# Another order of the up and down products in the second layer of a spectral mixture-of-experts kernel

## The chip, the cores and the metric

The kernel runs on one core of a Trainium2 chip. The metric is the device time of one execution in microseconds (us). The time of a kernel is the median of its runs.

## The reference, cut to what matters

The input `x` (8, 3072, 256) is filtered along its sequence in the frequency domain. A mixture of eight experts (one expert per token, hidden width 1024) follows, and then a dense second layer. Only this second layer is touched by the change:

```
def _moe2_ref(x, w_in, w_out):          # x: 24576 x 256
    h = np.maximum(x @ w_in, 0.0)       # 24576 x 2048
    return (h * h @ w_out)              # 24576 x 256
```

Everything is float32. The kernel keeps float32 accuracy by splitting each operand into a high and a low part and by forming three products of parts (high by high, low by high, high by low) for each product of the formula.

## The kernel before, in words

The program has three stages: the Fourier filter, the expert layer (the function that issues its steps is `steps_m`, which goes on with the second layer), and the second layer. The second layer works on 48 tiles of 512 tokens (`NTILE2`), and each tile in 8 **units** (`NU`) of 256 hidden columns, so there are 384 units. All engines follow one order, which is the order in which the generators `up2`, `split_h`, `down2` and `split_t` issue their instructions; each engine has its own queue and takes its instructions in that order.

**Up (`up2`, lines 892 to 925).** A unit's 256 x 512 block of `x @ w_in` is formed with a Strassen-like scheme from seven products of 128 x 128 by 128 x 256. Each product (`prod`, line 897) is three matmuls of 256 columns, 21 in all. I name a product by its PSUM tile and the number of its weight block: V0, G3, P1, V4, G6, V5, V2, in the order of the code. The three PSUM tiles are V (pool `psH`, two buffers; the trace calls it `ph`), G (pool `psX`, one buffer, `px`) and P (pool `psH2`, one buffer, `ph`). V4, V5 and V2 add onto what V0 left in V, and G6 adds onto what G3 left in G. Between two products onto the same tile the partial sum is copied out, and the next product waits for that copy:

- ScalarE copies V after V0 into `s1` (line 906), G after G3 into `p5` (line 908), V after V4 into `u2` (line 913), and V after V2 into `C[:, 2]` (line 921).
- VectorE adds P and `s1` into `C[:, 0]` (line 911), V (after V5) and `p5` into `C[:, 3]` (line 917), G (after G6) and `u2` into `C[:, 1]` (line 918).

So V4 waits for the copy `s1`, G6 for the copy `p5`, V5 for the copy `u2`, and V2 for the sum `C[:, 3]`. After V2 and its copy VectorE forms `q`, the square of the positive part of `C` (line 923, 1024 columns).

**Split (`split_h`, lines 927 to 934).** ScalarE casts `q` to the high part `hh` (line 930), and VectorE forms the low part `hl` (line 932).

**Down (`down2`, lines 936 to 961).** 24 matmuls of 256 columns add the unit's part of `h*h @ w_out` onto two PSUM banks (`py`). The sum over a tile's 8 units stays in these banks; behind the last unit ScalarE copies it out (line 951) and GpSimd scatters it to the output (line 954).

**The order before (lines 1055 to 1072).** In step n the up products of unit n, the split of unit n-1 and the down matmuls of unit n-2 are interleaved in four parts. On TensorE a step is

```
V0 G3 | 3 down | P1 V4 | 6 down | G6 V5 | 9 down | V2 | 6 down
```

that is 45 matmuls. `split_h` is issued in parts 1 and 2, and one step of `split_t` (lines 858 to 890, the split of the next tile's input, spread over four units of a tile) at the end of a step. The loads of a later tile (`load_t`) go through SyncE's DMA queue at unit 2 of each tile.

Of the kernel before, what the change touches and what calls it, by code (L numbers as in the profile page):

```python
# [17 lines left out]
ALU = mybir.AluOpType  # L18
# [84 lines left out]
def spectral_moe_kernel(ctx: ExitStack, tc: tile.TileContext, x, filt_r, filt_i, w_gate, w_og, w1, w2,  # L103
                        w_in, w_out, c_ma, c_mi, c_mb, c_mb2, c_sg, c_cum, out):
    nc = tc.nc
# [608 lines left out]
    def py_tiles(t):  # L714
        return [pl["psY2" if t % 2 and "psY2" in pl else "psY"].tile([128, TT], F32, name=f"py{h}") for h in range(2)]
# [82 lines left out]
    def up(t, f):  # L798
        xh, xl = X[t]
        w = width[t]  # L800
        h1, l1 = (a[:, 0] for a in W[t, f // 2])
        f2 = f % 2
        ps = ph_tile()[:, 0:w]
        n = 0
        for c in range(2):
            for a, b in ((h1, xh), (h1, xl), (l1, xh)):
                nc.tensor.matmul(ps, a[:, c, f2 * 128:(f2 + 1) * 128], b[:, c, 0:w], start=n == 0, stop=n == 5)  # L807
                n += 1
        hh = pl["hp"].tile([128, TT], F32R, name="hh")[:, 0:w]
        hl = pl["hp"].tile([128, TT], F32R, name="hl")[:, 0:w]  # L810
        nc.scalar.activation(hh, ps, AF.Relu)  # L811
        tick[:] = [hh[0:1, 0:1].bitcast(F32)]
        nc.vector.scalar_tensor_tensor(hl, ps, 0.0, hh.bitcast(F32), op0=ALU.max, op1=ALU.subtract)  # L813
        H[t, f] = hh, hl
# [77 lines left out]
    def up2(t, u):  # L892

        bh, bl, _ = X2[t]
        wsh, wsl = w2nd[0:2]

        def prod(ps, a, b, start):
            for n, (x, y) in enumerate(((wsh, bh), (wsh, bl), (wsl, bh))):
                nc.tensor.matmul(ps, x[:, u, a], y[:, b], start=start and n == 0, stop=n == 2, skip_group_check=True)  # L899

        bank = lambda name: pl[name].tile([128, TT], F32, name="px" if name == "psX" else "ph")[:, 0:256]
        V, G, P = bank("psH"), bank("psX"), bank("psH2")
        s1, p5, u2 = (pl["sp"].tile([128, 256], F32, name=n) for n in ("s1", "p5", "u2"))
        C = pl["cp"].tile([128, 4, 256], F32, name="C")
        prod(V, 0, 0, True)
        nc.scalar.copy(s1, V)
        prod(G, 3, 3, True)
        nc.scalar.copy(p5, G)
        yield
        prod(P, 1, 1, True)  # L910
        nc.vector.tensor_tensor(C[:, 0], P, s1, ALU.add)
        prod(V, 4, 4, False)
        nc.scalar.copy(u2, V)
        yield
        prod(G, 6, 2, False)
        prod(V, 5, 5, False)
        nc.vector.tensor_tensor(C[:, 3], V, p5, ALU.add)  # L917
        nc.vector.tensor_tensor(C[:, 1], G, u2, ALU.add)
        yield
        prod(V, 2, 6, False)  # L920
        nc.scalar.copy(C[:, 2], V)  # L921
        q = pl["cp"].tile([128, 4, 256], F32, name="q")
        nc.vector.scalar_tensor_tensor(q, C, 0.0, C, op0=ALU.max, op1=ALU.mult)  # L923
        H2[t, u] = q
        yield

    def split_h(t, u):
        q = H2[t, u]
        hh, hl = (pl["h2p"].tile([128, 4, 256], F32R, name=n) for n in ("hh2", "hl2"))
        nc.scalar.copy(hh, q)  # L930
        yield
        nc.vector.tensor_tensor(hl, q, hh.bitcast(F32), ALU.subtract)  # L932
        H2[t, u] = hh, hl
        yield

    def down2(t, u):

        hh, hl = H2[t, u]
        woh, wol = w2nd[2:4]
        if u == 0:  # L940
            Z[t] = [p.rearrange("p (c d) -> p c d", c=2) for p in py_tiles(t)]
        for m in range(24):
            k, i, c, n = m // 12, m // 6 % 2, m // 3 % 2, m % 3
            x, w = ((hh, woh), (hl, woh), (hh, wol))[n]
            nc.tensor.matmul(Z[t][k][:, c, :], x[:, 2 * i + k, c * 128:(c + 1) * 128], w[:, 2 * u + i, :],  # L945
                             start=u == 0 and m in (0, 12), stop=u == NU - 1 and m in (11, 23), skip_group_check=True)
            if u == NU - 1 and m in (11, 23):
                if k == 0:
                    Z[t].append(pl["oup"].tile([128, 4, D], F32, name="ou"))
                ou = Z[t][2]  # L950
                nc.scalar.copy(ou[:, 2 * k:2 * k + 2, :], Z[t][k])  # L951
                io = X2[t][2]
                for c in range(2 * k, 2 * k + 2):
                    nc.gpsimd.indirect_dma_start(out=outv[4 * t + c], out_offset=bass.IndirectOffsetOnAxis(ap=io[:, c:c + 1], axis=0),  # L954
                                                 in_=ou[:, c, :], in_offset=None)
            if m in (2, 8, 17):
                yield
        del H2[t, u]
        if u == NU - 1:
            del X2[t], Z[t]  # L960
        yield
# [3 lines left out]
    units2 = [(t, u) for t in range(NTILE2) for u in range(NU)]  # L965
# [3 lines left out]
    def step_1(t, f):  # L969

        last = t + 1 == KP
        if f == 5 and t + 2 == KP:
            start_t(KP)
        if f == 1 and t + 1 >= KP:
            for n in (t + 2, t + 3) if last else (t + 3,):
                if n < NMAIN:
                    start_t(n)
        if f == 1 and last:
            gather(KP)
        if f == 3 and t + 2 < NMAIN and t + 2 != KP:  # L980
            gather(t + 2)
        if f % 2 == 1:

            g = NQ * t + f // 2 + 2
            if NQ * KP <= g < NQ * NMAIN:
                split_w(*divmod(g, NQ))
            if NQ * KP <= g + 2 < NQ * NMAIN:
                load_w(*divmod(g + 2, NQ))
        if t + 1 < NMAIN:
            at = (4, 5, 7) if last else (2, 4, 6)  # L990
            if f == at[0]:
                scale_x(t + 1)
            if f == at[0] + 1:
                put_ids(t + 1)
            if f in at[1:]:
                turn_x(t + 1, at.index(f) - 1)
        elif f == 1:
            load_t(0)
            load_t(1)
        if f not in (1, 5) and dec and next(dec[0], 0) == 0:  # L1000
            dec.clear()
            dcs.close()
            pl["bp0"] = ctx.enter_context(tc.tile_pool(name="bp0", bufs=1))
            pl["bp0"].tile([128, 16], F32, name="pad0")
        if t + 1 == NMAIN and f >= 3:
            if f == 3:
                first.append(split_t(0))
            next(first[0], None)

    def extra(t):  # L1010

        start_t(t)
        gather(t)
        for q in range(3):
            load_w(t, q)
        scale_x(t)
        put_ids(t)
        turn_x(t, 0)
        turn_x(t, 1)
        for f in range(NF + 1):  # L1020
            if f < NF:
                if f % 2 == 0:
                    split_w(t, f // 2)
                    if f == 0:
                        load_w(t, 3)
                up(t, f)
            if f:
                down(t, f - 1)

    def rest(t):  # L1030

        if t < NTILE1:
            with tc.If(used[0] > slot[t - KP]):
                extra(t)
                rest(t + 1)
# [3 lines left out]
    def steps_m():  # L1039
        for n in range(len(jobs) + LAG1):  # L1040
            if n < len(jobs):
                t, f = jobs[n]
                up(t, f)
                step_1(t, f)
            if n >= LAG1:
                down(*jobs[n - LAG1])
            yield
        used.append(nc.values_load(usedi[0:1, 0:1], min_val=0, max_val=NTILE_T))
        with tc.If(used[0] > NTILE_T - NX):
            extra(NMAIN)  # L1050
            rest(NMAIN + 1)
        m1.close()
        xgs.close()
        open_m2()
        st = iter(())
        for n in range(len(units2) + 2):
            g = up2(*units2[n]) if n < len(units2) else iter(())
            t, u = units2[min(n, len(units2) - 1)]
            d = down2(*units2[n - 2]) if n >= 2 else iter(())
            for part in range(4):  # L1060
                next(g, None)
                if part == 0 and 0 < n <= len(units2):
                    sh = split_h(*units2[n - 1])
                if part in (1, 2) and n:
                    next(sh, None)
                next(d, None)
            if u == 2 and t + 2 < NTILE2:
                load_t(t + 2)
            if u == 3 and t + 1 < NTILE2:
                st = split_t(t + 1)  # L1070
            next(st, None)
            yield
# [43 lines left out]
    m = steps_m()  # L1116
# [4 lines left out]
    for i, k in enumerate(order):  # L1121
# [3 lines left out]
        n = done["a"]  # L1125
# [62 lines left out]
```

## Time and profile before

| | |
|---|---|
| median of 3 runs | 3807.01 us (3805.06 to 3810.75) |
| the profiled execution's own time | 3809.94 us |
| its span, first to last instruction | 3808.2 us |
| TensorE busy in the span | 98% |
| VectorE, ScalarE, GpSimd busy | 72%, 52%, 16% |
| mean granted TensorE clock | 0.997 |

The second layer fills the time from 1777 us to the end. TensorE is always busy there by its records, which says little, because a matmul's record (some 0.28 us) is longer than the distance from its start to the next one's start (some 0.115 us): matmuls overlap. What has to be read is that distance, called the **pitch** below.

### The profile page before, as it was taken

What the parts mean: (1) busy time and instruction counts of PE and PEld (TensorE: products, weight loads), DVE (VectorE), ACT (ScalarE), POOL (GpSimd) and SP (SyncE); (2) the same over time, 40 slices, a digit from 0 to 9 for tenths busy, and PEclk for the clock granted to TensorE, in tenths of its full rate; (3) what the DMA queues carried; (4) which work ended last, traced back from release to release, by engine and by line L of the source; (5) the groups of instructions that cost most, each with busy time, mean ns of one, the idle gap of its engine ahead of it and who ended that gap; (6) DMA issues with size and microseconds to landing.
All of it is one profiled execution on the core that took longest, in us unless ns stands there. A gap on an engine that the chain in (4) does not pass through costs nothing.

```text
span 3808.2 us, 73021 instructions
## 1 busy us (share of the span) xinstructions
PE 3750.1 (98%) x27156; PEld 3501.1 (92%) x27156; DVE 2759.2 (72%) x5024; ACT 1966.4 (52%) x3896; POOL 607.0 (16%) x641
## 2 busy tenths in 40 slices
PE   8999999999999999999999999999999999999998
PEld 7888877888888888888999999999999999999998
DVE  6677685678878875656777777777777777777775
ACT  6466473354545454554555555555555555555554
POOL 3477574000000000000011001000100110011001
PEclk9999999999999999999999999999999999999999
DMA  6333322455555554543000100010000001000100
GB/s 193 101 114 116 105 81 95 149 161 165 174 159 176 165 165 154 158 159 95 24 26 27 29 23 29 23 29 23 29 24 28 24 29 29 23 26 26 29 18 18
DMA packets 259756, 306.63 MB, mean 81 GB/s; under 512 B 74721, under 2 KB 203202, under 8 KB 259394
## 3 DMA queue, kind: packets, MB, share of 16 engines
q1 hardware_dynamic: 239936, 249.75, 21.6%
q0 software_dynamic: 18432, 51.93, 3.8%
q8 instruction: 214, 3.51, 0.4%
q14 instruction: 148, 1.21, 0.1%
q10 hardware_dynamic: 1026, 0.23, 0.0%
HBM read 221.63 MB, written 80.19 MB: 79 GB/s over the span
## 4 chain that ended last, share of the span: by engine, by line
PE 84%; issue 10%; DVE 2%; POOL 1%; DMA 1%; ACT 1%; another core or an unknown queue 0%; DVEq 0%; POOLq 0%; ACTq 0%; SPq 0%
PE py L945 22%; PE ph L899 14%; PE ph L807 14%; PE py L824 14%; PE px L899 6%; PE o L360 3%; PE p L380 3%; PE o L394 2%; PE p L281 2%; PE p L334 1%; PE p L338 1%; PE p L309 1%; POOL out_dram L954 1%; PE px L787 1%; DMA xt<-in_x_dram 0%
## 5 line engine op out<-in xcount | busy, mean ns | idle before, releaser
L945 PE MATMUL py<-woh,hh 128*128 128x256 f32 x3072 | 857.2, 279 | 0.0
L945 PE MATMUL py<-woh,hl 128*128 128x256 f32 x3072 | 852.8, 278 | 0.4 <-DVE hl L932 0.4
L945 PE MATMUL py<-wol,hh 128*128 128x256 f32 x3072 | 852.9, 278 | 0.0
L954 POOL DMA_INDIRECT out_dram<-ou,ix x192 | 213.2, 1110 | 2912.9 <-ACT ou L951 2869.0
L945 PEld LDWEIGHTS py<-woh,hl 128*128 128x128 f32 x3072 | 579.9, 189 | 0.9 <-DVE hl L932 0.8
L945 PEld LDWEIGHTS py<-woh,hh 128*128 128x128 f32 x3072 | 579.9, 189 | 0.0
L945 PEld LDWEIGHTS py<-wol,hh 128*128 128x128 f32 x3072 | 576.3, 188 | 0.0
L899 PE MATMUL ph<-bh,wsh 128*128 128x256 f32 x1920 | 540.9, 282 | 5.9 <-DMA ytd<-yt 4.6
L811 ACT ACTIVATE hh<-ph 128x512 fp32r<-128x512 f32 (+1 forms) x464 | 248.7, 536 | 574.8 <-PE ph L807 548.8
L899 PE MATMUL ph<-bl,wsh 128*128 128x256 f32 x1920 | 537.1, 280 | 0.0
L899 PE MATMUL ph<-bh,wsl 128*128 128x256 f32 x1920 | 536.7, 280 | 0.0
L923 DVE SCALAR_TENSOR_TENSOR q<-C 128x1024 f32<-128x1024 f32 x384 | 470.5, 1225 | 6.4 <-ACT C L921 6.4
L932 DVE TENSOR_TENSOR hl<-q,hh 128x1024 fp32r<-128x1024 f32 x384 | 467.1, 1216 | 1.1 <-ACT hh L930 1.1
L813 DVE SCALAR_TENSOR_TENSOR hl<-ph,hh 128x512 fp32r<-128x512 f32 (+1 forms) x464 | 283.3, 611 | 252.0 <-ACT hh L811 244.2
L917 DVE TENSOR_TENSOR C<-ph,p 128x256 f32<-128x256 f32 x384 | 163.6, 426 | 412.8 <-ACT hh L930 402.5
L921 ACT COPY C<-ph 128x256 f32<-128x256 f32 x384 | 143.4, 373 | 532.4 <-PE ph L899 500.2
L930 ACT CAST hh<-q 128x1024 fp32r<-128x1024 f32 x384 | 402.8, 1049 | 1.3 <-DVE q L923 1.3
L899 PEld LDWEIGHTS ph<-bh,wsh 128*128 128x128 f32 x1920 | 362.3, 189 | 7.1 <-issue 4.7
L899 PEld LDWEIGHTS ph<-bl,wsh 128*128 128x128 f32 x1920 | 360.9, 188 | 0.0
L899 PEld LDWEIGHTS ph<-bh,wsl 128*128 128x128 f32 x1920 | 360.8, 188 | 0.0
L824 PE MATMUL py<-hh,wh 128*128 128x512 f32 (+1 forms) x928 | 336.6, 369 | 0.0
L807 PE MATMUL ph<-xh,wh 128*128 128x512 f32 (+1 forms) x928 | 335.2, 361 | 0.0
(265 smaller groups left out, 8045.4 us busy)
## 6 DMA issues: line engine op xcount, KB each, us to landing
r<-in_moe_w_dram SPq DMA_DIRECT2D x440, 256.0 KB
xt<-in_x_dram SPq DMA_DIRECT2D x48, 512.0 KB
r<-ytd SPq DMA_DIRECT2D x48, 512.0 KB
xg<-srt SPq DMA_DIRECT2D x41, 544.0 KB
ytd<-yt SPq DMA_DIRECT2D x41, 512.0 KB
xg<-srt SPq DMA_DIRECT2D x17, 272.0 KB
ytd<-yt SPq DMA_DIRECT2D x17, 256.0 KB
raw<-in_moe_w_in_dram SPq DMA_DIRECT2D x16, 256.0 KB
```

Source lines behind the costliest of these rows:

```text
L807: nc.tensor.matmul(ps, a[:, c, f2 * 128:(f2 + 1) * 128], b[:, c, 0:w], start=n == 0, stop=n == 5)
L811: nc.scalar.activation(hh, ps, AF.Relu)
L813: nc.vector.scalar_tensor_tensor(hl, ps, 0.0, hh.bitcast(F32), op0=ALU.max, op1=ALU.subtract)
L824: nc.tensor.matmul(Y[t][h], a[:, f % 2, h * 128:(h + 1) * 128], b, start=f == 0 and i == 0, stop=f == NF - 1 and i == 2, skip_group_check= ...
L899: nc.tensor.matmul(ps, x[:, u, a], y[:, b], start=start and n == 0, stop=n == 2, skip_group_check=True)
L917: nc.vector.tensor_tensor(C[:, 3], V, p5, ALU.add)
L921: nc.scalar.copy(C[:, 2], V)
L923: nc.vector.scalar_tensor_tensor(q, C, 0.0, C, op0=ALU.max, op1=ALU.mult)
L930: nc.scalar.copy(hh, q)
L932: nc.vector.tensor_tensor(hl, q, hh.bitcast(F32), ALU.subtract)
L945: nc.tensor.matmul(Z[t][k][:, c, :], x[:, 2 * i + k, c * 128:(c + 1) * 128], w[:, 2 * u + i, :], start=u == 0 and m in (0, 12), stop=u == ...
L954: nc.gpsimd.indirect_dma_start(out=outv[4 * t + c], out_offset=bass.IndirectOffsetOnAxis(ap=io[:, c:c + 1], axis=0), in_=ou[:, c, :], in_o ...
```

## The change

The generator `up2` yields at more places, `down2` yields after 6 and after 15 of its 24 matmuls instead of after 3, 9 and 18, and the last three pieces of a unit (V2, the copy `C[:, 2]`, the square `q`) are issued in the next step, each behind a piece of the next unit (`old` is the generator of the unit before). The sum `C[:, 1]` is now issued before `C[:, 3]`. In the first step that has down matmuls (n == 2) their first six stand between G3 and P1; in all others the first two groups of down follow each other. A step's order on TensorE becomes

```
V0 (V2 of the unit before) G3 P1 V4 G6 | 15 down | V5 | 9 down
```

Every matmul, copy and sum of before is still issued, once.

```
--- before.py
+++ after.py
@@ up2
         prod(V, 0, 0, True)
         nc.scalar.copy(s1, V)
+        yield
         prod(G, 3, 3, True)
         nc.scalar.copy(p5, G)
         yield
         prod(P, 1, 1, True)
         nc.vector.tensor_tensor(C[:, 0], P, s1, ALU.add)
+        yield
         prod(V, 4, 4, False)
         nc.scalar.copy(u2, V)
-        yield
         prod(G, 6, 2, False)
+        nc.vector.tensor_tensor(C[:, 1], G, u2, ALU.add)
+        yield
         prod(V, 5, 5, False)
         nc.vector.tensor_tensor(C[:, 3], V, p5, ALU.add)
-        nc.vector.tensor_tensor(C[:, 1], G, u2, ALU.add)
         yield
         prod(V, 2, 6, False)
+        yield
         nc.scalar.copy(C[:, 2], V)
+        yield
         q = pl["cp"].tile([128, 4, 256], F32, name="q")
         nc.vector.scalar_tensor_tensor(q, C, 0.0, C, op0=ALU.max, op1=ALU.mult)
@@ down2
-            if m in (2, 8, 17):
+            if m in (5, 14):
                 yield
@@ steps_m
         st = iter(())
+        none = iter(())
+        old = none
         for n in range(len(units2) + 2):
-            g = up2(*units2[n]) if n < len(units2) else iter(())
+            g = up2(*units2[n]) if n < len(units2) else none
             t, u = units2[min(n, len(units2) - 1)]
-            d = down2(*units2[n - 2]) if n >= 2 else iter(())
-            for part in range(4):
-                next(g, None)
-                if part == 0 and 0 < n <= len(units2):
-                    sh = split_h(*units2[n - 1])
-                if part in (1, 2) and n:
-                    next(sh, None)
+            d = down2(*units2[n - 2]) if n >= 2 else none
+            next(g, None)
+            next(old, None)
+            next(g, None)
+            next(old, None)
+            if n == 2:
                 next(d, None)
+            next(g, None)
+            next(old, None)
+            sh = split_h(*units2[n - 1]) if 0 < n <= len(units2) else none
+            next(g, None)
+            next(sh, None)
+            if n != 2:
+                next(d, None)
+            next(d, None)
+            next(g, None)
+            next(sh, None)
+            next(d, None)
+            old = g
```

## Rows read from the trace of the kernel before

**Rows 1.** Page's busy times; a stretch: busy of PE, PEld, DVE, ACT, POOL; clock; DMA.

```profile
PE 3750.1 (98%) x27156; PEld 3501.1 (92%) x27156; DVE 2759.2 (72%) x5024; ACT 1966.4 (52%) x3896; POOL 607.0 (16%) x641
...
2500.00:3000.00 500.00, 500.00 (x4290) 500.00 (x4289) 369.39 (x573) 259.95 (x549) 53.02 (x48) 1.00 0.09 27
```

**Rows 2.** The chain of waits over one unit: start, us, what; from V0 on.

```profile
2505.66 0.35 PE ph L899 x3
2506.02 0.35 PE px L899 x3
2506.37 0.35 PE py L945 x3
2506.72 0.69 PE ph L899 x6
2507.42 0.68 PE py L945 x6
2508.10 0.35 PE px L899 x3
2508.46 0.35 PE ph L899 x3
2508.81 1.06 PE py L945 x9
2509.87 0.35 PE ph L899 x3
2510.23 0.68 PE py L945 x6
```

**Rows 3.** The timeline, same unit: last matmul of G3, copy p5, first weights of G6.

```profile
2506.09 0.28 PE L899 MATMUL px<-bh,wsl 128*128 128x256 f32 x1
...
2506.46 0.37 ACT L908 COPY p<-px 128x256 f32<-128x256 f32 x1
...
2507.83 0.19 PEld L899 LDWEIGHTS px<-bh,wsh 128*128 128x128 f32 x1
```

**Rows 4.** The timeline in unit 1, before any down: V0's last matmul, s1, V4.

```profile
1782.58 0.28 PE L899 MATMUL ph<-bh,wsl 128*128 128x256 f32 x1
...
1782.90 0.37 ACT L906 COPY s<-ph 128x256 f32<-128x256 f32 x1
...
1783.26 0.28 PE L899 MATMUL ph<-bh,wsl 128*128 128x256 f32 x1
1783.32 0.19 PEld L899 LDWEIGHTS ph<-bh,wsh 128*128 128x128 f32 x1
1783.38 0.33 PE L899 MATMUL ph<-bh,wsh 128*128 128x256 f32 x1
...
1783.54 0.28 PE L899 MATMUL ph<-bl,wsh 128*128 128x256 f32 x1
...
1783.78 0.28 PE L899 MATMUL px<-bh,wsh 128*128 128x256 f32 x1
```

**Rows 5.** The timeline where a V2 waited for its sum: one of three such units.

```profile
1816.85 0.19 PEld L899 LDWEIGHTS ph<-bh,wsh 128*128 128x128 f32 x1
...
1817.08 0.28 PE L899 MATMUL ph<-bl,wsh 128*128 128x256 f32 x1
...
1817.19 0.28 PE L899 MATMUL ph<-bh,wsl 128*128 128x256 f32 x1
...
1817.30 0.28 PE L945 MATMUL py<-woh,hh 128*128 128x256 f32 x1
```

**Rows 6.** The page's costliest groups: VectorE's and ScalarE's long steps of a unit.

```profile
L923 DVE SCALAR_TENSOR_TENSOR q<-C 128x1024 f32<-128x1024 f32 x384 | 470.5, 1225 | 6.4 <-ACT C L921 6.4
L932 DVE TENSOR_TENSOR hl<-q,hh 128x1024 fp32r<-128x1024 f32 x384 | 467.1, 1216 | 1.1 <-ACT hh L930 1.1
...
L917 DVE TENSOR_TENSOR C<-ph,p 128x256 f32<-128x256 f32 x384 | 163.6, 426 | 412.8 <-ACT hh L930 402.5
...
L930 ACT CAST hh<-q 128x1024 fp32r<-128x1024 f32 x384 | 402.8, 1049 | 1.3 <-DVE q L923 1.3
```

More of the change, by code (lines that the diff above doesn't have):

```diff
@@ L911, in up2 @@
         nc.vector.tensor_tensor(C[:, 0], P, s1, ALU.add)
+        yield
         prod(V, 4, 4, False)
         nc.scalar.copy(u2, V)
+        prod(G, 6, 2, False)
+        nc.vector.tensor_tensor(C[:, 1], G, u2, ALU.add)
         yield
-        prod(G, 6, 2, False)
         prod(V, 5, 5, False)
         nc.vector.tensor_tensor(C[:, 3], V, p5, ALU.add)
-        nc.vector.tensor_tensor(C[:, 1], G, u2, ALU.add)
         yield
         prod(V, 2, 6, False)
+        yield
         nc.scalar.copy(C[:, 2], V)
+        yield
         q = pl["cp"].tile([128, 4, 256], F32, name="q")
```

## The prediction

> **What bounds the kernel now.** I read the busy times first, then one long stretch, then the chain of waits, then the timeline. In the stretch from 2500 to 3000 us TensorE starts 4290 matmuls, one per 116.6 ns, at a granted clock of 1.00, which is the 2.4 GHz level, while VectorE is busy 74% and ScalarE 52% of the time [rows 1]. The chain of waits names nothing but matmuls there, 45 per unit, in 5.25 us (2505.66 to 2510.23 + 0.68) [rows 2]. So no wait bounds the second layer; the pitch of the matmuls does, and it is all that a new order can win.
>
> The pitch has two values. Six down matmuls take 0.68 us from 2507.42, and again from 2510.23: 113.3 ns each, the fast pitch. The nine from 2508.81 take 1.06 us: 117.8 ns, the slow pitch [rows 2]. All are 256 columns wide, with operands of the same kinds, so it is not the work that differs. Read along the unit, the pitch changes at each step from a down group to an up group and nowhere else: V0 starts a slow stretch that lasts through three down matmuls, P1 brings the fast pitch back, G6 starts the next slow stretch, and V2 ends it [rows 2]. I take that as a rule: **each switch from down to up flips the pitch**. Price of a slow stretch, with the three matmuls that bring the fast pitch back: 2505.66 to 2507.42 is 1.76 us for 15 matmuls, where 15 x 113.3 ns are 1.70, so 60 ns for nine slow matmuls; 2508.10 to 2510.23 is 2.13 us for 18, where the fast pitch gives 2.04, so 90 ns for fifteen [rows 2]. That is about 5 ns per slow matmul and 15 ns for the way back. The check: 45 x 113.3 = 5.10 us, plus 60, plus 90, is the unit's 5.25.
>
> **The change, part by part.**
>
> *Fewer switches.* A step has two flips in place of four, at V5 and at V0. If V0 to G6 and the 15 down matmuls are fast, only V5 and the nine behind it are slow: twelve, 12 x 5 + 15 = 75 ns. The unit would be 5.10 + 0.075 = 5.175 us, 72 ns less than 5.247 (I take 45 x 116.6 ns [rows 1]).
>
> *G6 behind its copy.* Before, 15 matmuls (three down, P1, V4, six down) stand between G3 and G6. Now it is six, P1 and V4. The chain that G6 must wait out is in the trace: G3's last matmul starts at 2506.09 and the copy p5 at 2506.46, 0.37 later, and takes 0.37 [rows 3]; from the end of such a copy to the weight load that waits for it are 0.05 us (1782.90 + 0.37, then 1783.32) [rows 4]. Together 0.79. G6's weight load would come naturally 6 x 113.3 = 0.68 us after G3's last matmul. So TensorE stands for 0.11 us in every unit. The trace has this distance once: in unit 1, with no down matmuls yet, V4 follows V0 after six matmuls (G3, P1). Its weight load comes at 1783.32 where the matmul ahead started at 1783.26, and the matmul after is at 1783.54, 0.16 behind V4's first in place of 0.11 [rows 4]. There the copy started only 0.31 us after the matmul (1782.58 to 1782.90) [rows 4]; in the steady units it is 0.37. Bounds of this wait: 0.05 us [rows 4] and 0.11 us [rows 3]; I take 0.11, the row of the same copy. Nothing else fills it: behind G6's load in TensorE's queue stand 15 down matmuls with all their inputs ready, and they are held with it, as is everything later. ScalarE and VectorE shift along, and they have room.
>
> *What pitch follows that wait.* Where V2 waited in full (weights at 1816.85), the next matmuls came at 1817.08, 1817.19 and 1817.30, the fast pitch [rows 5]. Where V4 waited half as long, the next two came 0.24 us apart (1783.54 to 1783.78), slow [rows 4]. A wait of 0.11 us is a full one (the load comes later than the matmul would have), so I take fast, and no more loss than the wait.
>
> *The other waits,* each with its cover. V4 waits for s1: nine matmuls between, 1.02 us against 0.79. V5 waits for u2: 18 between. V2 waits for VectorE's sum behind V5: 12 between, 1.36 us, against 0.37 + 0.43 [rows 6] + 0.05. The copy of V2 now stands behind p5, so it costs p5 nothing. Counted from G3's last matmul: sum of P at 0.7 to 1.1 us, `q` to 2.4, `hh` to 3.5, the sum of V5 (matmuls at 3.2, sum from 3.6) to 4.0, `hl` to 5.2 [rows 6]; the down matmuls want them in the next step, at 5.3 + 1.1 = 6.4. Cover 1.2 us. In the unit where `split_t` puts four subtractions behind `hl` (some 4 x 0.43 us), `q` and `hh` come 0.8 us later, and the cast behind them (1.05 us) may hold the next s1 by 0.2 to 0.3 us, which leaves V4 some 0.03 us short: 47 tiles, at most 2 us in all. The scatters and SyncE's loads keep their places; GpSimd is busy 16% [rows 1].
>
> *Start and end.* V2 of unit 0 no longer holds unit 1, but `q` of units 0 and 1 comes later for the first down matmuls; at the end six down matmuls fewer cover the last unit's chain (6 x 0.113 = 0.7 us lost). I put both together at 0, within 1 us.
>
> **Sum.** Unit: 5.10 + 0.075 + 0.115 = 5.290 us, 43 ns more than before. Steps 3 to 383 have it, 381 of them: +16.4 us. The profiled execution took 3809.94 us, 2.9 above the median; 3809.9 + 16.4 = 3826.3, and against the median of 3807.0 it is **3823.4 us**, slower by 0.43%.
>
> **Rivals.**
>
> *The flips go the other way,* so that V0 to G6 and the 15 down matmuls are slow: 33 slow matmuls, 33 x 5 + 15 = 180 ns. The wait is then shorter, 0.79 - 6 x 0.118 = 0.08. Unit 5.10 + 0.18 + 0.08 = 5.36: +43 us, 3850. It decides if the wait leaves the slow pitch, as in unit 1 [rows 4]; against it stands the full wait of rows 5.
>
> *The pitch hangs on something else than the switches* (a group's addresses), so it stays at 116.6 ns on average and only the wait is new: 0.79 - 6 x 0.1166 = 0.09 us, +34 us, 3841. For it: I infer the rule from one pattern of groups. Against: the four flips of every unit. [...]
>
> *All fast but for the wait:* if V5's switch does not bring the slow pitch, the unit is 5.10 + 0.115 = 5.215, 32 ns less: -12 us, 3795. While the wait stands, no pitch gives more.
>
> *The wait costs nothing* and the fewer switches win: -72 ns x 381 = -27 us, 3780. This is the faster case, in one mechanism: G6's weights would have to be loaded before p5 is done, so that only the matmul waits. Then the matmul, due 0.79 us after G3's last one (7 x 113.3), comes just as p5 is done; it decides once the load gets ahead by 0.1 us. Against it: in unit 1 the load itself came late, with the matmul behind it [rows 4]. [...]
>
> *The two cancel:* a wait of 0.05 us, as in rows 4, with the 75 ns of slow matmuls gives 5.225, -8 us; a wait of 0.07 gives no change.
>
> **How the numbers follow.** About 0.2% (8 us) is what a measurement of this kernel can tell from no change. My forecast, +10 to +22 us: 0.42. Pitch independent of the switches, or slow after part of the waits, +22 to +38: 0.14. Flips the other way, +38 to +45: 0.12. All fast but for the wait: 0.10. No wait: 0.10. Cancelled: 0.12. Slower by over 0.2% is 0.42 + 0.14 + 0.12 = 0.68; faster 0.20; the same 0.12. The range from 3794 to 3850 leaves out the case without a wait and the edge of the reversed one. The forecast's own range is 3817 to 3829.
>
> **What would show it.** In the profile after, ScalarE's copy p5 should be what ends an idle of G6's weight load, some 380 times, with 0.3 us or less between the matmul ahead and the load; the chain should show 33 fast and 12 slow matmuls per step; V0 of one unit to V0 of the next should be 5.29 us. I am wrong if G6's load comes 0.11 us behind the matmul ahead (no wait), if the nine down matmuls behind V5 take 1.02 us and not 1.06, or if the fifteen take 1.77 us and not 1.70.

## The result, and the profile after

The changed kernel takes 3838.73 us (median of 4 runs, 3834.85 to 3839.97) where the kernel before takes 3808.88 (4 runs): a ratio of 1.0079, with a 95% interval of 1.0066 to 1.0092. It is slower by 29.9 us. The forecast was 3823.4, 16.4 us slower: the direction and the wide range (3794 to 3850) held, the size was off by nearly half, and the time lies outside the forecast's own range of 3817 to 3829.

All of it lies in the second layer. In the profiled executions its first up matmul starts at 1777.4 us before and 1776.1 after, its last down matmul at 3797.4 and 3827.1: 2019.9 us against 2051.1, 31.1 us more. From one V0 to the next a unit takes 5.248 us before and 5.327 after, on the mean of 377 units; 381 x 0.079 us are 30.1 us. (Counts of units, here and below, are of those that start between 1800 and 3808 us, unless steps are named.)

The busy times of the page after, which answer to [rows 1]:

```profile
PE 3781.0 (99%) x27156; PEld 3523.5 (92%) x27156; DVE 2758.9 (72%) x5024; ACT 1996.7 (52%) x3896; POOL 620.1 (16%) x641
```

And the stretch from 2500 to 3000 us of the kernel after: us, then busy time (count) of PE, PEld, DVE, ACT, POOL, granted clock, DMA share, GB/s.

```profile
2500.00:3000.00 500.00, 499.91 (x4228) 497.54 (x4227) 363.36 (x565) 264.00 (x542) 56.64 (x48) 1.00 0.09 27
```

The same number of matmuls in all, the same granted clock of 1.00 (the 2.4 GHz level), but 4228 matmuls in the stretch where there were 4290: 118.3 ns each, not 116.6. TensorE looks busier than before (99%), which shows again that its busy share says little here.

The chain of waits over two units of the kernel after (start, us, what), which answers to [rows 2]. A `ph` group of six right behind nine `py` is V0 and the V2 of the unit before:

```profile
2504.91 0.34 PE px L899 x3
2505.25 0.68 PE ph L899 x6
2505.93 0.46 PE px L899 x3
2506.39 1.77 PE py L949 x15
2508.16 0.35 PE ph L899 x3
2508.51 1.02 PE py L949 x9
2509.53 0.71 PE ph L899 x6
2510.24 0.35 PE px L899 x3
2510.60 0.70 PE ph L899 x6
2511.30 0.43 PE px L899 x3
2511.73 1.70 PE py L949 x15
2513.43 0.36 PE ph L899 x3
2513.78 1.06 PE py L949 x9
```

Read the two units side by side. In the first, G3 (0.34) and P1, V4 (0.68 for six) are fast, and G6 takes 0.46 instead of 0.34, because it waits. Then the 15 down matmuls are slow (1.77), and the nine behind V5 fast (1.02). The second is the mirror: V0 to V4 are slow (0.71, 0.35, 0.70), G6 takes 0.43 instead of 0.35, the 15 down matmuls are fast (1.70), and the nine slow (1.06). So the two switches flip the pitch, as forecast, and the wait is there, as forecast. But the wait itself also turned the pitch over, in both units, where the forecast took fast behind it.

The timeline of these two waits: G3's last matmul, the copy p5, V4's last matmul, G6's first weights and second matmul, then the same of the next unit. It answers to [rows 3].

```profile
2504.98 0.28 PE L899 MATMUL px<-bh,wsl 128*128 128x256 f32 x1
...
2505.34 0.37 ACT L909 COPY p<-px 128x256 f32<-128x256 f32 x1 [0.31 <-PE px L899]
...
2505.66 0.28 PE L899 MATMUL ph<-bh,wsl 128*128 128x256 f32 x1
...
2505.77 0.19 PEld L899 LDWEIGHTS px<-bh,wsh 128*128 128x128 f32 x1
...
2505.99 0.28 PE L899 MATMUL px<-bl,wsh 128*128 128x256 f32 x1
...
2510.32 0.28 PE L899 MATMUL px<-bh,wsl 128*128 128x256 f32 x1
...
2510.69 0.37 ACT L909 COPY p<-px 128x256 f32<-128x256 f32 x1 [0.25 <-PE px L899]
...
2511.11 0.19 PEld L899 LDWEIGHTS px<-bh,wsh 128*128 128x128 f32 x1
...
2511.34 0.28 PE L899 MATMUL px<-bl,wsh 128*128 128x256 f32 x1
```

G6's weights come 0.79 us after G3's last matmul in both units (2504.98 to 2505.77, 2510.32 to 2511.11), which is the sum of the prediction. Because V0 to V4 are fast in the one and slow in the other, the same chain costs 0.108 us in the one and 0.08 in the other (median of 138 and of 239 units; it is read from G6's first matmul to its second).

Sorted by the pitch of V0 to V4, of the 15 down matmuls and of the nine, nearly all of the 377 units are of three kinds: fast, slow, fast (137 units, median 5.313 us); slow, fast, slow (136 units, 5.313 us); slow, slow, fast (102 units, 5.347 us). The kind that the forecast was made for (fast, fast, slow, at 5.290) occurs once. Two of the prediction's own signs of being wrong came: 15 down matmuls at 1.77 us and nine at 1.02, each in at least 239 of the 377 units.

### The profile page after: what moved, and what is told of

Its sections match the earlier page's. It is cut to its first block, busy times and chain, and to the rows that moved or that the text cites. A ratio compares the mean times of both kernels' runs of the same rounds, so it can differ in the third digit from the quotient of the medians.

```text
span 3838.0 us, 72547 instructions
## 1 busy us (share of the span) xinstructions
PE 3781.0 (99%) x27156; PEld 3523.5 (92%) x27156; DVE 2758.9 (72%) x5024; ACT 1996.7 (52%) x3896; POOL 620.1 (16%) x641
## 4 chain that ended last, share of the span: by engine, by line
PE 38%; issue 14%; POOL 2%; ACT 0%; DVE 0%; POOLq 0%; ACTq 0%
PE py L949 20%; PE ph L899 12%; PE px L899 6%; POOL out_dram L958 2%; DVE q L927 0%; ACT p L909 0%; DVE hl L936 0%; ACT hh L934 0%; POOLq L1200 0%; ACT ou L955 0%; DVE C L920 0%; ACT C L924 0%; POOLq L958 0%; DVE C L912 0%; ACTq L955 0%
## 5 line engine op out<-in xcount | busy, mean ns | idle before, releaser
L958 POOL DMA_INDIRECT out_dram<-ou,ix x192 | 225.3, 1173 | 2932.0 <-ACT ou L955 1735.3
L906 ACT COPY s<-ph 128x256 f32<-128x256 f32 x384 | 143.5, 374 | 433.9 <-PE ph L899 369.8
```

## The experiments

The time of the kernel before differs between the chips on which the runs below were made (3809.4, 3793.6, 3795.1 and 3805.1 us). So ratios are given, and the length of the second layer in the trace, which does not hold the stages ahead of it.

**G3 first: the wait taken away.** In the step, V2 of the unit before goes behind G3:

```
             next(g, None)
-            next(old, None)
             next(g, None)
             next(old, None)
+            next(old, None)
```

> G3 and its copy p5 are issued before V2 of the unit before, so nine matmuls (1.02 us) stand between G3 and G6 where the chain through p5 takes 0.79 us. Theory (each switch from down to up flips the pitch, and G6's wait costs its own time and also puts the pitch wrong): no wait, the same pattern in every unit, two flips; with V0 to G6 and 15 down matmuls fast and 12 matmuls slow the unit is 5.175 us, some 3782 us in all, 27 us under the kernel before. If this start gives the other pattern, 33 slow matmuls, the unit is 5.28 us and the time some 3821 us. Rival A (the pitch belongs to a group of matmuls, not to the switches): the time is the same whatever the start, so this run and the next agree. Rival B (only the wait matters, the mean pitch stays 116.6 ns): unit 5.247 us, the time of the kernel before.

Measured: 3788.03 us, a ratio of 0.9943 (0.9926 to 0.9959): faster than both kernels. The second layer is 2002.4 us long, 17.6 less than before. The chain of waits over two units of this one run, the first at 2509.76:

```profile
2509.76 0.35 PE ph L899 x3
2510.11 0.34 PE px L899 x3
2510.45 1.02 PE ph L899 x9
2511.47 0.34 PE px L899 x3
2511.81 1.70 PE py L949 x15
2513.51 0.35 PE ph L899 x3
2513.87 1.06 PE py L949 x9
```

and another, at 2192.67:

```profile
2192.67 0.35 PE ph L899 x3
2193.02 0.35 PE px L899 x3
2193.38 1.06 PE ph L899 x9
2194.44 0.35 PE px L899 x3
2194.79 1.77 PE py L949 x15
2196.56 0.35 PE ph L899 x3
```

The first has up matmuls and 15 down matmuls at the fast pitch, and nine at the slow pitch; the second the reverse. The same instructions, in the same order, on the same tiles: so the pitch does not belong to a group of matmuls (rival A falls), and the mean pitch does not stay (rival B falls). The first pattern has 325 units, with a median of 5.173 us (the theory said 5.175); the second 42 units, 5.267 us (5.28). What keeps the time above the 3782 of the theory is that the pattern changes within the run, and where it changes, V4 has waited for s1. It does so in 32 units, by 0.15 us on the mean.

**The same without the special first step.** The six down matmuls between G3 and P1 at n == 2 are gone:

```
-            if n == 2:
-                next(d, None)
...
-            if n != 2:
-                next(d, None)
+            next(d, None)
             next(d, None)
```

> As the run with G3 first, but the first step that has down matmuls is like all others: its first six down matmuls no longer stand between G3 and P1, which is one switch from down to up less at the start and no other difference in 384 units. Theory (switches flip the pitch): with no wait to disturb it, one flip less reverses the pitch of every later unit, so if the run with G3 first has 12 slow matmuls per unit (5.175 us), this one has 33 (5.28 us), some 40 us longer, and the other way round. Rival A (the pitch belongs to the groups) and rival B (only the wait matters): the same time within 1 us.

Measured: 3786.75 us, 0.9946 (0.9930 to 0.9963), the same as the run with G3 first. The expected difference of 40 us is not there. It is no case for the groups either: this trace has 350 units of the first pattern and 17 of the second. Both runs begin with some units of the second pattern, until a wait of V4 (in unit 11 of the run with G3 first, 0.08 us; in unit 9 of this one, some 0.01 us); the start is forgotten there. So this run could not tell what it was made for.

**The changed kernel without its special first step.** The same edit on the changed kernel.

> The changed kernel without its special first step (no six down matmuls between G3 and P1 at n == 2). Theory: the wait at G6 sets the pitch anew in nearly every unit, so a flip at the start is forgotten: the same mixture of units (5.31 and 5.35 us), 3838 us within 4. Rival (the start decides the pitch for good also with the wait): a time that differs by 10 us or more.

Measured in one run: 3844.84 us, second layer 2059.2 us, 8 longer than the changed kernel. A miss of both expectations in a small way: it is not within 4 us, and it is not the start that decides for good. The units are of the same three kinds, in other shares: 347 of 376 are slow, slow, fast (5.347 us). In the trace of the changed kernel, after a wait that begins in the slow pitch, G6's second matmul starts 195 or 196 ns behind its first in 136 of the 138 units where the fast pitch follows, and 198 to 200 ns behind it in 100 of the 102 where the slow one does. Two nanoseconds separate the kinds, and what moves them stays open.

**P1 first: a longer wait.** In `up2`, P1 and its sum go ahead of G3 and its copy:

```
+        prod(P, 1, 1, True)
+        nc.vector.tensor_tensor(C[:, 0], P, s1, ALU.add)
+        yield
         prod(G, 3, 3, True)
         nc.scalar.copy(p5, G)
         yield
-        prod(P, 1, 1, True)
-        nc.vector.tensor_tensor(C[:, 0], P, s1, ALU.add)
-        yield
```

> The changed kernel with P1 ahead of G3, so that three matmuls and not six stand between G3 and G6: the wait grows by 3 x 0.113 = 0.34 us, to 0.45 us in every unit. By the sum of waits the time grows by 381 x 0.34 = 130 us to some 3968 us. What it tells apart is the pitch behind a wait that is long in all units: if a wait always flips the pitch, units alternate between fast and slow ahead of the wait and every 15 down matmuls are of the other pitch than V0 to V4; if a long wait always leaves the slow pitch, every unit has slow 15 and, after two switches, slow V0 to V4 (60 slow-unit matmuls gone from the alternating pattern, units all alike, some 10 us longer); if it always leaves the fast pitch, all units have fast 15, slow V5 and nine, fast V0 to V4.

Measured in one run: 3954.84 us, 13 under the expected 3968, second layer 2164.0. A unit is 5.620 us, and 355 of 357 are of one kind: fast, fast, slow. The chain of waits at one G6:

```profile
2509.10 0.18 issue
2509.28 0.61 PE px L899 x3
2509.89 1.70 PE py L949 x15
```

The wait of 0.45 us leaves the fast pitch (1.70 for 15). (The edit also puts the copy C2 ahead of p5; what that order alone does is tried below.) That is the kind of unit the forecast took, with a wait four times as long. Its price is the forecast's sum, too: 5.10 + 0.075 + 0.445 = 5.62.

**p5 later: another longer wait.** One narrow copy more on ScalarE, ahead of p5:

```
+        nc.scalar.copy(p5[:, 0:64], G[:, 0:64])
         nc.scalar.copy(p5, G)
```

> The changed kernel with a suspected wait made longer: ScalarE copies 64 columns of G into p5 first and then all 256 as before, which puts some 0.15 to 0.25 us more between G3 and G6. By the sum of waits the time grows by 381 x 0.2 = 76 us. What it tells apart is the pitch behind the wait: with 0.11 us the changed kernel has a slow pitch behind the wait whenever it was fast ahead of it (137 of 137 units), with 0.45 us (P1 ahead of G3) it is fast behind it (355 of 357). If the length of the wait decides, a wait of 0.3 us gives one kind of unit throughout, and shows on which side of a border it lies; if it hangs on chance, both kinds are mixed.

Measured in one run: 3904.67 us (the kernel before: 3793.62 on this chip), second layer 2130.1. A unit is 5.533 us, and all 363 are slow, slow, fast:

```profile
2509.00 0.62 PE px L899 x3
2509.62 1.77 PE py L950 x15
```

Here G6's wait begins in the slow pitch, costs some 0.27 us and leaves the slow pitch, every time. So it is not "a wait always flips". The outcomes so far: 0.108 us from the fast pitch, slow (137 of 138 units; the other one waited 0.39 us, and fast followed); 0.45 us from the fast pitch, fast; 0.27 us from the slow pitch, slow; and 0.08 us from the slow pitch lies at a border, and both follow. Nor is it "long leaves fast, short leaves slow": 0.08 us can leave fast, and three waits of V2 in the last two runs below, 0.52 us each from the fast pitch, left slow twice and fast once. No length was tried in all units from both pitches, so how much the pitch it begins in matters, apart from the length, is not shown.

**ScalarE's order undone.** C2 ahead of p5, the part of the change that the order V, G, V names:

```
             next(g, None)
             next(old, None)
-            next(g, None)
             next(old, None)
+            next(g, None)
```

> The changed kernel with one part of it undone: ScalarE copies V of the unit before (C2) ahead of G (p5), in the order V, V, G. V2 ends three matmuls ahead of G3, and a copy can start some 0.35 us after the one before it started, so p5 starts some 0.01 us later than in the changed kernel. Theory: ScalarE's order is worth next to nothing, 381 x 0.01 = 4 us, unless the pitch behind the wait changes with it; 3838 to 3850 us. Rival (the order is what keeps the wait small): p5 a whole copy later, 0.37 us per unit, some 3980 us.

Measured in one run: 3830.11 us beside 3793.62 for the kernel before; second layer 2056.4 us, 5.3 longer than in the changed kernel. The order is worth little, as expected; what it moves is the shares of the kinds (285 of 375 slow, slow, fast), not the wait, which has the medians of the changed kernel (from G6's first matmul to its second 196 or 198 ns where the wait begins in the slow pitch, 222 where it begins in the fast).

**21 and 3 down matmuls.** On the run with G3 first:

```
-            if m in (5, 14):
+            if m in (5, 20):
```

> As the run with G3 first, with 21 and 3 down matmuls where that has 15 and 9. Theory (a switch from down to up flips the pitch, and a slow stretch costs 15 ns and 5 ns per slow matmul): the slow stretch is now V5 and three down matmuls, 6 x 5 + 15 = 45 ns, so the regular unit falls from the 5.173 us of the run with G3 first to some 5.143, and the time by 381 x 0.03 = 11 us, to some 3776 us. If the pitch starts on the other foot, 39 matmuls are slow and the unit is 5.30 us, some 3829 us. Rival (the cost of a slow stretch is fixed, at the switch): unit 5.173, the time of the run with G3 first, 3788. Second rival: V2, now nine matmuls behind V5 (1.02 us, chain 0.85), waits for VectorE's sum where that is late; then a wait stands at V2 in many units.

Measured: 3775.29 us, 0.9957 (0.9941 to 0.9973), no better than the run with G3 first by the ratio. Two things cancel. The regular unit is 5.147 us, as expected (5.143), 26 ns less than with 15 and 9. But V4 now waits in all 47 tiles, 0.25 us each, some units behind such a wait have the slow pattern, and a unit is 5.194 us on the mean. The waits of this run (engine, line, who was waited for: us in total, times, longest us) name it:

```profile
PEld ph L899 <- ACT s L906: 8.2, 41, 0.2
```

**The split of the next tile issued early.** On the run with 21 and 3:

```
             next(g, None)
+            if u == 3 and t + 1 < NTILE2:
+                st = split_t(t + 1)
+            next(st, None)
             next(sh, None)
...
-            if u == 3 and t + 1 < NTILE2:
-                st = split_t(t + 1)
-            next(st, None)
             yield
```

> As the run with 21 and 3, with the step of split_t issued in front of ScalarE's cast hh instead of at the end of a step. In the run with G3 first V4 waits once per tile (0.15 to 0.2 us, in 42 of 47 tiles) for s1, which stands behind the 1.05 us cast of split_t on ScalarE; ScalarE idles 0.9 us ahead of hh. Theory: the cast fills that idle time, V4's waits go, and with them the stretches of units on the wrong foot that follow some of them: some 45 x 0.18 + what the wrong foot costs = 8 to 12 us less than the run with 21 and 3, about 3766 us. Rival: VectorE's four subtractions now stand ahead of the sum behind V5 and V2 waits for that instead, once per tile: no gain.

Measured: 3759.49 us (four runs, 3758.80 to 3760.09), a ratio of 0.9909 (0.9893 to 0.9926): the fastest version, 16 us under the run with 21 and 3. No V4 waits any more. 373 of 375 units are of one kind, 5.147 us, and the second layer is 1983.7 us long, 36.3 less than before. One unit of it, from its 21 down matmuls on, and the next one's up matmuls:

```profile
2506.82 2.38 PE py L949 x21
2509.20 0.35 PE ph L899 x3
2509.56 0.35 PE py L949 x3
2509.91 0.35 PE ph L899 x3
2510.27 0.34 PE px L899 x3
2510.61 1.02 PE ph L899 x9
2511.63 0.34 PE px L899 x3
```

21 fast down matmuls (2.38, 113.3 ns each), six slow matmuls, and all else fast.

**One switch more, two switches more.** In the fastest version, at one step or at two:

```
-            if n == 2:
+            if n in (2, 200):
                 next(d, None)
...
-            if n != 2:
+            if n not in (2, 200):
                 next(d, None)
```

> The fastest version (G3 first, 21 and 3, split early), in which 373 of 375 units show one pattern with no wait, with one edit in one of 384 units: at step 200 the first six down matmuls stand between G3 and P1, which is one switch from down to up more. Theory (a switch flips the pitch and nothing sets it back): units up to 199 keep 5.147 us, and from 200 on V0 to G6 and 21 down matmuls are slow, V5 and three fast: 39 x 5 + 15 = 0.21 less what is fast, some 5.29 us per unit; 184 x 0.146 = 27 us longer. Rival (the pitch belongs to the groups, or settles by itself): units after 200 are like those before it within a few units, and the time is the same within 1 us.

> As the run with one more switch, with a second one at step 220. Theory: the second flips the pitch back, so only the 20 units from 200 to 219 are slow: 20 x 0.146 = 3 us longer than the fastest version, and units 220 to 383 at 5.147 us again. Rival (a switch at a new place leaves the slow pitch, it does not flip): units from 220 on stay at 5.29 us, 27 us longer.

Measured, one more: 3787.43 us as the median of 8 runs, but at three levels: one run at 3759.60, five from 3786.5 to 3788.9, two at 3813.9 and 3814.9, some 27 us apart, which is the expected 184 x 0.146. In the trace of one of the five, the 197 units from step 3 to 199 have the slow pattern (5.293 us), and the 182 after step 200 the fast one: the theory's units with the two sides exchanged. Two more: 3760.67 (2 runs), and in its trace the fast pattern throughout. The two do not settle it, because the added switch brings a wait: the six down matmuls come before their hl, and stand 0.3 us. In the run with two more switches that wait turned the fast pitch slow and the added switch turned it back, at both steps.

**One switch less, two switches less.** The clean form of the same question:

```
+        few = (200,)
...
+            if n - 1 in few:
+                next(g, None)
             next(old, None)
             next(old, None)
...
-            next(g, None)
+            if n - 1 not in few:
+                next(g, None)
...
+            if n in few:
+                next(d, None)
             next(g, None)
             next(sh, None)
-            next(d, None)
+            if n not in few:
+                next(d, None)
```

> The added switch of the earlier runs came with a wait of its own (a first down matmul that stood 0.3 us for hl), which can change the pitch as well. So here a switch is taken away, without a wait: in the fastest version, at step 200 alone, all 24 down matmuls stand ahead of V5, so V0 of step 201 follows V5 directly and there is one switch from down to up less; in step 201 P1 goes ahead of V2 of the unit before, so that V2 still has nine matmuls behind V5. Theory (a switch flips the pitch): the pattern of every unit behind step 200 is the reverse of the one before it, 5.147 us on one side and 5.293 on the other, with no wait in between. Rival (the groups have their pitch, or the wait did it): the same unit on both sides.

> As the run with one switch less, with a second one taken away at step 216. Theory: the pattern is reversed from step 200 to step 216, 16 units, and is the first one again behind it. Rival (the groups have their pitch): one pattern throughout. Second rival (a missing switch leaves the slow pitch): the pattern behind step 216 is that of steps 201 to 216.

Measured, one less: 3827.35 us in one run, beside 3805.11 for the kernel before. The chain of waits around step 200, which is the group of 24:

```profile
2833.05 0.35 PE ph L899 x3
...
2833.75 1.06 PE ph L899 x9
...
2835.17 2.83 PE py L949 x24
2838.00 0.69 PE ph L899 x6
...
2839.03 1.02 PE ph L899 x9
...
2840.39 2.38 PE py L949 x21
2842.77 0.36 PE ph L899 x3
2843.13 0.35 PE py L949 x3
...
2844.18 1.02 PE ph L899 x9
```

Up to there the nine up matmuls take 1.06 us and the 24 down matmuls 2.83, the slow pitch. V5 behind them turns it fast, V0 follows without a switch, and from then on the same nine take 1.02 and the 21 take 2.38, with no wait in between. The pattern is reversed by one missing switch. Two units later V2 waits some 0.5 us and the slow pattern is back for the rest. So 370 of 378 units have the slow pattern, at 5.293 us, and this run is slower than the kernel before, although nothing waits at G6. With two switches less the trace shows the fast pattern from step 201 to step 216 in all units but one, and the slow pattern on both sides, as the theory has it. It is the weaker evidence of the two: two waits of V2, some 0.5 us each, stand in between, and the unit of the first is the one that is slow. 3824.04 us, in one run.

Up to step 200 the last four runs have the program of the fastest version, and so show where its pattern comes from. In its trace the units from 3 to 8 are of the slow pattern. In unit 9 the first two matmuls of V4 start 121 and 126 ns behind the ones ahead of them, where the slow pitch is 118, and from there on every unit is of the fast pattern. A delay of about the same size is followed there by the fast pattern with two switches more and with two less (there until a wait of V2 at step 19), and by the slow one with one switch more. With one switch less the first units are fast, and V4 of unit 9, some 0.05 us late, turns them slow.

## Why the prediction was right in direction and short in size

- **The pitch, not waits, bounds the layer.** Right: the changed kernel differs by the pitch and one wait. Of the versions without that wait those with mostly fast units are faster than before, and those with mostly slow units (one and two switches less) are slower.
- **Each switch from down to up flips the pitch.** Right, and shown: by both patterns in the run with G3 first, and by the run with one switch less. Counted in all 14 traces from unit 3 on, 11,361 of the 11,377 switches without a wait beside them flip it. The other 16 are switches to V5 that leave the slow pitch slow, each in a unit in which TensorE had waited. The price of a slow stretch was right too: twelve slow matmuls were put at 75 ns, and the regular units are 5.173 us for 5.175, then 5.147 for 5.143 with six. The Trainium skill ("TensorE: Matmul & The Clock Gate", section "Back-to-back issue gap") gives N/2.4 + 2.5 ns for a matmul by itself, by which I estimate 109 ns for 256 columns, and says that in a stream of weight loads and matmuls both set the distance; it has no second distance for one width. The traces have 113.3 and 117.8 ns for the same matmuls, so here the measurement decides.
- **G6's wait of 0.11 us.** Right: 0.108 us from the fast pitch (and 0.08 from the slow one, as the reversed rival had it). The rival in which the weights are loaded ahead of the wait did not come: the load itself starts 0.79 us behind G3's last matmul. That TensorE pulls weight loads ahead of matmuls in flight, as the Trainium skill has it ("TensorE: Matmul & The Clock Gate", section "Part 2: What happens when you issue a matmul"), is not seen across this wait. One sign of the prediction failed all the same: the view of waits names p5 at G6's load in 6 units and not in some 380, so the wait had to be read from the starts.
- **What pitch follows the wait.** Wrong, and this is the term that was mis-sized. "A wait of 0.11 us is a full one, so I take fast" rested on waits of V2, where the switch to V2 had flipped the pitch anyway. Measured, 137 of 138 such waits leave the slow pitch. The following 15 down matmuls are slow, the next V0 starts on the other foot, and the wait there ends either way. A unit costs 5.327 us, not 5.290: 79 ns over before in place of 43.
- **The other covers.** V4's cover for s1 was put at some 0.03 us short once per tile. In the changed kernel no V4 waits, and the large waits are at G6: in 6 units p5 starts late and G6's weights come 0.28 to 0.29 us later than usual. What held p5 there stays open. In another order, with G3 first, it is V4 that waits, 0.15 us in 32 units, and the early split takes that wait away. So the place was wrong for this kernel; for that other one it would have been right, and the size too small by a factor of five.
- **The sum.** 381 x 0.079 = 30.1 us against 31.1 us measured in the layer. The prediction named "slow after part of the waits" as a rival, at +22 to +38 us with a chance of 0.14 that it shared with another; that is what came. That the direction held was in part luck: the forecast's kind of unit occurs once, and the kinds in its place happen to be dearer.

## What to carry to other kernels

Where the matmuls of a tight loop are the bound, read their start-to-start distance group by group before believing the busy share; a change of order can be worth 2% of a stage with no wait involved. When an order is changed, count the matmuls between a partial sum and the next product onto it, and compare with the whole chain through the copy (here 0.79 us, so seven fast matmuls at the least). A wait that is forecast should be priced with what it does to the pace behind it, and rows of the same kind of wait, without another cause beside it, are needed for that.

## What the runs showed of the hardware that was not expected

- In the second layer matmuls of one shape run at one of two distances, 113.3 or 117.8 ns, and where nothing waits every step from a down group to an up group turns one into the other, for hundreds of units on end. Why the step does so was not tried. Two are not all there are: in the expert layer of the kernel before, matmuls of the same shape start 120 ns apart (1764.07, 1764.19, 1764.31 us), at the same granted clock of 1.00.
- A wait of TensorE changes that distance or not, and where its length hardly varies, reliably so: 355 of 357, 363 of 363 and 137 of 138 units in three cases. At a border (196 or 198 ns from G6's first matmul to its second) it goes both ways. What sets the border stays open.
- So a kernel whose waits end with its first units keeps, for the whole layer, whatever pattern they leave, and in the trace of the fastest version that pattern was turned over at a delay of some 10 ns in one unit. The fastest version had the good one in four runs of four; a version that differs from it in one of 384 steps took 3759.6, 3787 or 3814 us in eight, and the two with switches less, on another chip, ran nearly all of the layer in the slow one. Its 0.9909 is what was measured, and not a promise for each start.
